# Another order for the first transfers of an attention-and-MLP kernel, and decoding of weights from its first step

## The chip, the cores and the metric

The kernel runs on one NeuronCore of a Trainium2 chip, as one launch. The metric is the device time of the launch in microseconds (us). TensorE (PE) multiplies matrices, VectorE (DVE) and ScalarE (ACT) work on whole tiles, GpSimd (POOL) only sets up constants here, and SyncE (SP) issues most of the transfers. PEld is the loading of weights into the PE array.

## What is computed

The inputs are q, k, v and a complex decay a, of 4 batches, 8 heads, 768 positions and 48 channels. A state of 48x48 per head is decayed and added to at every position, and two MLPs follow on the 3072 tokens of width 384, with a hidden width of 2048:

```
scale = min(|a|, 0.999) / (|a| + 1e-6);  a = a * scale          # complex
for t in range(768):
    S = a[t] * S + outer(k[t], v[t]);  y[t] = q[t] @ real(S)
x = y as (3072, 384)
x = softplus(x @ w_in1) @ w_out1
out = elu(x @ w_in2) @ w_out2
```

The MLP weights arrive as float64 and are used as pairs of float32 parts (high and low), so each product is three matmuls.

## The kernel before

**Attention.** The sequence is cut into 12 units of 256 positions (3 to a batch). For a unit u, `load_a` fetches the real and imaginary decays, `load_qk` q and k, `load_v` v by halves. `norm` (L143) makes the scale of the decays: squares on ACT, a sum on DVE, Ln and Exp on ACT, then DVE and ACT in turn. `prep` (L175) forms the running products W of the decays on DVE, first `W<-ar` and `W<-ai` (L183, L185). `qk` (L232) multiplies them into q (QP, the tile `big<-W,qr`) and divides k by them (KP, `big<-W,tmp`, L267). KP is stored to DRAM as `kd` (L271) and read back in another layout as `KN` (L327); PE waits for KN before it updates the state (L395). `chunks` (L799) issues scores (L334), the causal mask on DVE (tile P, L340), outputs (L358, L361) and a relay into the layout of the first MLP (L384). What it leaves is X[u], as a high and a low part (`xh` and `xl`, L404 and L405).

**Weights.** A granule is a 128x384 float64 block, 384 KB; the first MLP has 32 of them, the second 32 more. `w_load` (L487) fetches one, an even one from w_in, an odd one from w_out. `w_step` (L507) decodes one: on ACT an Abs and an Exp that test the range (L445, L446), on DVE three integer operations (L449, L451, L452), then ACT copies the high part (L404) and DVE subtracts it (L405). Here granule g is written g0, g1 and so on.

**Order.** A generator `stream()` hands out the attention in steps. Until X[0] is there, one weight granule is handed out with each step once `step > S0`, until G0 = 22. Thereafter the first MLP runs in 8 pieces per unit (n = 0 to 95, `a_s1` at L528, `a_elem` at L538 with DVE's L545 and L550) with attention handed out in between, and from unit 11 on the second MLP follows. The order in which these are issued is a first order only: a scheduler that plays the program through with costs of its own moves the instructions of each engine. The engines then work in that order, and each waits in it. SP issues in order too: its transfers take eight completion semaphores in turn, so a transfer waits for the one eight places ahead.

Before, the first transfers are the decays of unit 0, its q and k, two halves of v, the decays of unit 1, and then granules 0 to 7 (L938 to L944).

Of the kernel before, what the change touches and what calls it, by code (L numbers as in the profile page):

```python
# [411 lines left out]

CH0 = 7
DLY = 2
S0 = 6
STEP = 2000
STEPS = 4
G0 = 22
# [6 lines left out]
LA = 8  # L425
# [328 lines left out]
def body(tc, q, k, v, a_re, a_im, w_in1, w_out1, w_in2, w_out2, out):  # L754
    nc = tc.nc
    keep = tc.tile_pool(name="keep", bufs=1)
    with keep as keep:
        fine = quick(tc, keep, q, k, v, a_re, a_im, w_in1, w_out1, w_in2, w_out2, out)
        n = nc.values_load(fine[0:1, 0:1], min_val=0, max_val=128)
        with tc.If(n < 128):  # L760
            general(tc, q, k, v, a_re, a_im, (w_in1, w_out1, w_in2, w_out2), out)


def quick(tc, keep, q, k, v, a_re, a_im, w_in1, w_out1, w_in2, w_out2, out):
    nc = tc.nc
    with ExitStack() as ctx:
# [13 lines left out]
        net = Net(tc, ctx, flags[:, 28:92], bank, ((w_in1, w_out1), (w_in2, w_out2)))  # L780
# [4 lines left out]
        A = Attn(tc, actx, flags, bank, net, q, k, v, a_re, a_im)  # L785
# [136 lines left out]
        def adv(ns):  # L922
# [3 lines left out]
            for _ in range(STEPS):  # L926
# [5 lines left out]
                try:  # L932
# [2 lines left out]
                    due = A.vec.ns  # L935
                    return

        A.load_a(0)  # L938
        A.load_qk(0)
        A.load_v(0)  # L940
        A.load_v(1)
        A.load_a(1)
        for net.top in range(LA):
            net.w_load(net.top)  # L944
        while 0 not in X:
            next(st)
            if net.g < G0 and step > S0:
                net.w_step()
# [130 lines left out]
```

## Time and profile before

| | us |
|---|---|
| median of 3 runs | 1166.83 |
| lowest and highest of them | 1163.89, 1168.22 |
| the profiled execution | 1162.61 |
| its span, from first to last instruction | 1160.8 |
| PE, DVE, ACT busy | 1001.1, 810.4, 667.2 |

Busy times overlap, and instructions that follow each other on an engine overlap a little too. The profile also names for each idle stretch what ended it, and follows a chain of waits back from the last instruction; rows called "issue" in it are time in which nothing that the profile shows was waited for.

### The profile page before, as it was taken

What the parts mean: (1) busy time and instruction counts of PE and PEld (TensorE: products, weight loads), DVE (VectorE), ACT (ScalarE), POOL (GpSimd) and SP (SyncE); (2) the same over time, 40 slices, a digit from 0 to 9 for tenths busy, and PEclk for the clock granted to TensorE, in tenths of its full rate; (3) what the DMA queues carried; (4) which work ended last, traced back from release to release, by engine and by line L of the source; (5) the groups of instructions that cost most, each with busy time, mean ns of one, the idle gap of its engine ahead of it and who ended that gap; (6) DMA issues with size and microseconds to landing.
All of it is one profiled execution on the core that took longest, in us unless ns stands there. A gap on an engine that the chain in (4) does not pass through costs nothing.

```text
span 1160.8 us, 18255 instructions
## 1 busy us (share of the span) xinstructions
PE 1001.1 (86%) x7106; PEld 933.2 (80%) x7106; DVE 810.4 (70%) x1521; ACT 667.2 (57%) x1207; POOL 2.2 (0%) x20
## 2 busy tenths in 40 slices
PE   0015988898999797997999899999999999999997
PEld 0014888888988797897999899999999999999996
DVE  3997999798987889796989978983434343333332
ACT  4735865565746565474656578974545454454443
POOL 0000000000000000000000000000000000000000
PEclk9996999999998899898999999999999999999999
DMA  7536262343634435472546365530101000000000
GB/s 205 182 116 161 91 171 76 89 140 88 175 96 116 118 108 175 98 204 56 179 108 210 83 205 187 160 117 1 55 1 55 1 1 28 1 28 1 29 1 30
DMA packets 101823, 114.51 MB, mean 99 GB/s; under 512 B 49760, under 2 KB 78944, under 8 KB 101728
## 3 DMA queue, kind: packets, MB, share of 16 engines
q1 hardware_dynamic: 90272, 105.40, 31.6%
q10 hardware_dynamic: 11456, 7.87, 2.2%
q8 instruction: 57, 0.93, 0.3%
q14 instruction: 38, 0.31, 0.1%
HBM read 77.86 MB, written 35.39 MB: 98 GB/s over the span
## 4 chain that ended last, share of the span: by engine, by line
PE 58%; DMA 16%; DVE 13%; ACT 8%; issue 4%; SPq 2%; ACTq 0%; DVEq 0%
PE b L525 49%; DMA kd<-big 4%; DMA KN<-kd 4%; DVE big L28 3%; PE b L334 3%; DVE tmp L28 3%; PE b L395 2%; PE b L358 2%; DMA wr<-in_moe_w_out_dram 1%; ACT w L446 1%; ACT w L445 1%; DMA wr<-in_moe_w_in_dram 1%; PE b L361 1%; DVE W L28 1%; DMA kT<-dk 1%
## 5 line engine op out<-in xcount | busy, mean ns | idle before, releaser
L525 PE MATMUL b<-xh,w 128*128 128x256 f32 (+1 forms) x1728 | 405.6, 328 | 32.3 <-ACT xh L404 25.3
L525 PEld LDWEIGHTS b<-xh,w 128*128 128x128 f32 x1728 | 293.9, 197 | 55.5 <-ACT xh L404 27.7
L525 PE MATMUL b<-xl,w 128*128 128x256 f32 (+1 forms) x864 | 278.9, 326 | 0.1
L525 PE MATMUL b<-gh,w 128*128 128x256 f32 x1152 | 213.4, 286 | 1.7 <-ACT gh L548 1.6
L525 PE MATMUL b<-w,gh 128*128 128x384 f32 x768 | 191.1, 335 | 0.0
L525 PEld LDWEIGHTS b<-gh,w 128*128 128x128 f32 x1152 | 176.9, 193 | 4.4 <-ACT gh L548 2.5
L525 PEld LDWEIGHTS b<-xl,w 128*128 128x128 f32 x864 | 167.5, 195 | 13.2 <-DVE xl L405 0.7
L584 DVE SCALAR_TENSOR_TENSOR t<-t,b 128x512 f32<-128x512 f32 x96 | 66.0, 687 | 151.1 <-ACT t L582 151.1
L525 PE MATMUL b<-gl,w 128*128 128x256 f32 x576 | 156.0, 286 | 1.4 <-DVE gl L550 1.4
L525 PEld LDWEIGHTS b<-w,gh 128*128 128x128 f32 x768 | 139.9, 188 | 7.8
L525 PE MATMUL b<-w,gl 128*128 128x384 f32 x384 | 124.2, 335 | 0.0
L581 ACT ACTIVATE t<-b 128x512 f32<-128x512 f32 x96 | 57.2, 597 | 111.1 <-PE b L525 110.3
L405 DVE TENSOR_TENSOR gl<-t,gh 128x512 fp32r<-128x512 f32 x96 | 66.4, 692 | 72.0 <-ACT gh L404 70.9
L525 PEld LDWEIGHTS b<-gl,w 128*128 128x128 f32 x576 | 106.5, 192 | 3.0 <-DVE gl L550 2.2
L404 ACT ACTIVATE gh<-t 128x512 fp32r<-128x512 f32 x96 | 60.6, 632 | 78.0 <-PE b L525 72.0
L541 ACT ACTIVATE t<-b 128x512 f32<-128x512 f32 x96 | 56.8, 593 | 66.5 <-PE b L525 56.2
L296 PE MATMUL b<-eye,big 128*96 128x128 f32 x112 | 19.3, 320 | 86.8 <-DVE big L28 86.5
L548 ACT ACTIVATE gh<-t 128x512 fp32r<-128x512 f32 x96 | 60.0, 627 | 55.5 <-PE b L525 37.2
L296 PEld LDWEIGHTS b<-eye,big 128*96 128x96 f32 x112 | 14.8, 147 | 88.5 <-issue 85.5
L525 PEld LDWEIGHTS b<-w,gl 128*128 128x128 f32 x384 | 71.7, 188 | 0.1
L550 DVE TENSOR_TENSOR gl<-t,gh 128x512 fp32r<-128x512 f32 x96 | 65.4, 685 | 8.1 <-ACT gh L548 7.0
L545 DVE SCALAR_TENSOR_TENSOR t<-b,t 128x512 f32<-128x512 f32 x96 | 65.5, 683 | 5.6 <-ACT t L543 5.4
(114 smaller groups left out, 1440.6 us busy)
## 6 DMA issues: line engine op xcount, KB each, us to landing
wr<-in_moe_w_in_dram SPq DMA_DIRECT2D x32, 384.0 KB
wr<-in_moe_w_out_dram SPq DMA_DIRECT2D x32, 384.0 KB
dq<-big SPq DMA_DIRECT2D x12, 768.0 KB
qT<-dq SPq DMA_DIRECT2D x36, 256.0 KB
kd<-big SPq DMA_DIRECT2D x12, 768.0 KB
KN<-kd SPq DMA_DIRECT2D x20, 384.0 KB
ar<-in_a_re_dram SPq DMA_DIRECT2D x12, 384.0 KB
ai<-in_a_im_dram SPq DMA_DIRECT2D x12, 384.0 KB
```

Of the source, the lines that this page charges most:

```text
L28: return f(*a, **kw)
L296: nc.tensor.transpose(out=ps[0:96, 128 * i:128 * i + 128], in_=W[:, 96 * (4 * g + i):96 * (4 * g + i) + 96], identity=self.eye)
L334: self.nc.tensor.matmul(out=sc[:, h, :], lhsT=KT[:, 4 * g + h, :], rhs=QT[:, 4 * g + h, :], start=(h == 0), stop=(h == 3), skip_group_chec ...
L404: nc.scalar.activation(out=hi, in_=x, func=AF.Copy)
L405: nc.vector.tensor_tensor(out=lo, in0=x, in1=hi.bitcast(F32), op=ALU.subtract)
L525: self.nc.tensor.matmul(out=out, lhsT=lhsT, rhs=rhs, skip_group_check=True, **kw)
L541: nc.scalar.activation(out=t, in_=h, func=AF.Abs)
L545: nc.vector.scalar_tensor_tensor(out=t, in0=h, scalar=0.0, in1=t, op0=ALU.max, op1=ALU.add)
L548: nc.scalar.activation(out=gh, in_=t, func=AF.Copy)
L550: nc.vector.tensor_tensor(out=gl, in0=t, in1=gh.bitcast(F32), op=ALU.subtract)
L581: nc.scalar.activation(out=t, in_=h, func=AF.Relu, scale=-1.0)
L584: nc.vector.scalar_tensor_tensor(out=t, in0=t, scalar=-1.0, in1=h, op0=ALU.add, op1=ALU.max)
```

## The change

The first transfers are issued in another order: granule 0, the decays of unit 0, granules 1 to 4, the decays of unit 1, granules 5 to 7, then q and k and two halves of v. And S0 is 0, so that decoding is handed out from the first step on. Nothing is added or left out.

```diff
-S0 = 6
+S0 = 0
...
+        net.w_load(0)
         A.load_a(0)
+        for net.top in range(1, 5):
+            net.w_load(net.top)
+        A.load_a(1)
+        for net.top in range(5, LA):
+            net.w_load(net.top)
         A.load_qk(0)
         A.load_v(0)
         A.load_v(1)
-        A.load_a(1)
-        for net.top in range(LA):
-            net.w_load(net.top)
```

What it moves is seen in three places. SP's first transfers (wr is a granule as it arrives, ar and ai are decays), before:

```order
L96 DMA ar_143<-in_a_re_dram 128x1x768
L96 DMA ai_145<-in_a_im_dram 128x1x768
L106 DMA qr_147<-in_q_dram 128x1x768
L106 DMA kr_149<-in_k_dram 128x1x768
L112 DMA V0_137<-in_v_dram 128x8x48
L112 DMA V1_139<-in_v_dram 128x8x48
L96 DMA ar_153<-in_a_re_dram 128x1x768
L96 DMA ai_155<-in_a_im_dram 128x1x768
L496 DMA wr_157<-in_moe_w_in_dram 128x3x128
```

and now:

```order
L496 DMA wr_143<-in_moe_w_in_dram 128x3x128
L96 DMA ar_145<-in_a_re_dram 128x1x768
L96 DMA ai_147<-in_a_im_dram 128x1x768
L494 DMA wr_149<-in_moe_w_out_dram 128x384
L496 DMA wr_151<-in_moe_w_in_dram 128x3x128
L494 DMA wr_153<-in_moe_w_out_dram 128x384
L496 DMA wr_155<-in_moe_w_in_dram 128x3x128
L96 DMA ar_157<-in_a_re_dram 128x1x768
L96 DMA ai_159<-in_a_im_dram 128x1x768
L494 DMA wr_161<-in_moe_w_out_dram 128x384
```

Granules 6 and 7, q, k and the two halves of v follow, and then granule 8. DVE's first instructions behind its memsets (tmp is the scale of unit 0, f and w are a granule in decoding), before:

```order
L28 SCALAR_TENSOR_TENSOR tmp_173<-tmp_173,tmp_174 128x768
L28 TENSOR_TENSOR tmp_174<-tmp_173,tmp_175 128x768
L28 SCALAR_TENSOR_TENSOR tmp_174<-tmp_174,tmp_175 128x768 x2
L449 TENSOR_SCALAR f_202<-wr_157 128x384
L28 SCALAR_TENSOR_TENSOR en_301<-en_301,en_302 128x768
L28 SCALAR_TENSOR_TENSOR tmp_173<-tmp_173,tmp_174 128x768
L451 SCALAR_TENSOR_TENSOR f_202<-wr_157,f_202 128x384
L449 TENSOR_SCALAR f_219<-wr_159 128x384
L28 TENSOR_TENSOR W_187<-ar_143,tmp_173 128x16x48
```

and now:

```order
L449 TENSOR_SCALAR f_179<-wr_143 128x384
L451 SCALAR_TENSOR_TENSOR f_179<-wr_143,f_179 128x384
L452 SCALAR_TENSOR_TENSOR f_179<-wr_143,f_179 128x384
L405 TENSOR_TENSOR w_178<-f_179,w_178 128x384
L28 SCALAR_TENSOR_TENSOR tmp_173<-tmp_173,tmp_174 128x768
L449 TENSOR_SCALAR f_193<-wr_149 128x384
L449 TENSOR_SCALAR f_206<-wr_151 128x384
L451 SCALAR_TENSOR_TENSOR f_193<-wr_149,f_193 128x384
L451 SCALAR_TENSOR_TENSOR f_206<-wr_151,f_206 128x384
L452 SCALAR_TENSOR_TENSOR f_193<-wr_149,f_193 128x384
L452 SCALAR_TENSOR_TENSOR f_206<-wr_151,f_206 128x384
L28 TENSOR_TENSOR tmp_174<-tmp_173,tmp_175 128x768
```

Five granules are decoded there ahead of `W<-ar`, where before there were three instructions of two granules. The third place is ACT's first instructions behind its table load (en is the scale of unit 1), before:

```order
L148 ACTIVATE tmp<-ar 128x768
L149 ACTIVATE tmp<-ai 128x768
L152 ACTIVATE tmp<-tmp 128x768
L153 ACTIVATE tmp,flags<-tmp 128x768
L156 ACTIVATE tmp<-tmp,flags 128x768
L148 ACTIVATE en<-ar 128x768
L159 ACTIVATE tmp<-tmp,flags 128x768
L149 ACTIVATE en<-ai 128x768
L445 ACTIVATE w<-wr 128x384
```

and now:

```order
L445 ACTIVATE w<-wr 128x384
L446 ACTIVATE w,flags<-w 128x384
L148 ACTIVATE tmp<-ar 128x768
L404 ACTIVATE w<-f 128x384
L149 ACTIVATE tmp<-ai 128x768
L445 ACTIVATE w<-wr 128x384
L446 ACTIVATE w,flags<-w 128x384
L152 ACTIVATE tmp<-tmp 128x768
L445 ACTIVATE w<-wr 128x384
L153 ACTIVATE tmp,flags<-tmp 128x768
L445 ACTIVATE w<-wr 128x384
L446 ACTIVATE w,flags<-w 128x384
```

The tests of the granules now stand between the steps of the scale of unit 0.

## Rows read from the trace of the kernel before

**Rows 1.** Page, parts 1 and 2: busy share of the span, and in 40 slices.
```profile
PE 1001.1 (86%) x7106; PEld 933.2 (80%) x7106; DVE 810.4 (70%) x1521; ACT 667.2 (57%) x1207; POOL 2.2 (0%) x20
...
PE   0015988898999797997999899999999999999997
...
DVE  3997999798987889796989978983434343333332
```

**Rows 2.** Windows: busy us of PE, PEld, DVE, ACT, POOL, clock, DMA share, GB/s.
```profile
23.40:80.40 57.00, 0.00 (x0) 0.00 (x0) 56.47 (x127) 31.87 (x82) 0.00 (x0) 1.00 0.48 163
80.40:117.50 37.10, 22.46 (x156) 17.74 (x156) 30.21 (x77) 20.81 (x44) 0.00 (x0) 0.73 0.64 172
117.50:188.40 70.90, 62.94 (x514) 57.78 (x514) 67.33 (x144) 48.63 (x93) 0.00 (x0) 0.95 0.38 107
188.40:780.00 591.60, 541.77 (x4552) 518.75 (x4553) 515.62 (x969) 381.58 (x691) 0.00 (x0) 0.95 0.48 137
...
sum 1137.40, PE 1001.13 PEld 933.17 DVE 806.42 ACT 659.07 POOL 0.00; mean PE 200.23 PEld 186.63 DVE 161.28 ACT 131.81 POOL 0.00
```

**Rows 3.** Timeline to 30 us: start, us, instruction, idle before it and its releaser.
```profile
0.83 0.80 SPq L96 DMA_DIRECT2D ar<-in_a_re_dram  x1
...
3.71 4.94 SPq L112 DMA_DIRECT2D V<-in_v_dram  x2
6.17 0.84 ACT L148 ACTIVATE tmp<-ar 128x768 f32<-128x768 f32 x1 [4.06 <-DMA ar<-in_a_re_dram]
8.69 5.08 SPq L96 DMA_DIRECT2D ar<-in_a_re_dram  x1
8.86 0.84 ACT L149 ACTIVATE tmp<-ai 128x768 f32<-128x768 f32 x1 [1.84 <-DMA ai<-in_a_im_dram]
...
18.78 0.84 ACT L148 ACTIVATE en<-ar 128x768 f32<-128x768 f32 x1 [4.22 <-DMA ar<-in_a_re_dram]
...
20.48 0.96 DVE L28 SCALAR_TENSOR_TENSOR tmp<-tmp 128x768 f32<-128x768 f32 x1 [5.97 <-ACT tmp L159]
...
23.44 0.36 DVE L449 TENSOR_SCALAR f<-wr 128x384 int32<-128x384 int32 x1 [2.00 <-DMA wr<-in_moe_w_in_dram]
...
27.06 0.95 DVE L28 TENSOR_TENSOR W<-ai,tmp 128x768 f32<-128x768 f32 x1
```

**Rows 4.** Windows, same columns: transfers of weights, and one of q alone.
```profile
25.00:30.00 5.00, 0.00 (x0) 0.00 (x0) 5.00 (x9) 5.00 (x15) 0.00 (x0) 1.00 1.05 373
...
70.00:71.00 1.00, 0.00 (x0) 0.00 (x0) 1.00 (x2) 1.00 (x3) 0.00 (x0) 1.00 0.48 187
```

**Rows 5.** Chain in order of time, to 80 us: start, us, what.
```profile
67.69 0.47 DVE f L451
68.15 0.27 DVE f L449
...
78.76 1.68 DVE big L28
```

**Rows 6.** Chain, behind 80 us: store and reload of unit 0.
```profile
80.46 6.13 DMA kd<-big
86.60 8.05 DMA KN<-kd
...
188.44 0.60 DVE t L545
```

**Rows 7.** Timeline of the first unit behind the reload: DVE and PE.
```profile
94.79 2.76 PE L395 MATMUL b<-V,KN 128*96 128x48 f32 x16 [6.83 <-DMA KN<-kd]
96.90 0.36 DVE L449 TENSOR_SCALAR f<-wr 128x384 int32<-128x384 int32 x1 [3.35 <-DMA wr<-in_moe_w_out_dram]
...
101.41 0.69 DVE L28 TENSOR_TENSOR P<-b,mask 128x512 f32<-128x512 f32 x1 [2.61 <-PE b L334]
```

**Rows 8.** Timeline, same: second half of unit 0 and the first matmul.
```profile
106.55 0.68 DVE L28 TENSOR_TENSOR P<-b,mask 128x512 f32<-128x512 f32 x1
...
117.54 1.65 PE L525 MATMUL b<-xh,w 128*128 128x256 f32 x6 [0.58 <-ACT xh L404]
```

## The prediction

> **What bounds the kernel now.** I read the shares of the span first. Over the whole, PE is busiest (86%), but the slices show two parts: in the last third PE is full and DVE at a third, while before that DVE is nearly full and in the first three slices, to 80 us, PE does nothing [rows 1]. A stage-by-stage table of busy time then says who sets the pace of the start. DVE is busy 56.5 of 57.0 us from 23.4 to 80.4, when the first keys are ready to be stored; 30.2 of 37.1 to the first MLP matmul at 117.5; and 67.3 of 70.9 to 188.4, where the first elementwise step of unit 1 stands [rows 2, 6, 8]. From there to 780 PE is busy 542 and DVE 516 of 592: both are near full, and the chain goes through both.
>
> Ahead of 23.4 us DVE is nearly idle. Of its 810.4 us in all, 806.4 lie behind that point, so 4.0 are ahead of it and 19.4 are idle [rows 1, 2]. The timeline shows why: the decays of unit 0 arrive at 6.2 and 8.9, then two halves of v hold up SP's issue (4.94 us for the two, and 5.08 for the transfer behind them). ACT, in its order, stands at the square of the decays of unit 1 until 18.8, with the last step of unit 0's scale behind it, for which DVE waits 5.97 us; and the first granule is there only at 23.4 [rows 3]. So the start is bound by when things arrive, and from 23.4 on by DVE.
>
> **The change, part by part.** No instruction is added or removed; what counts is what lies in the idle 19.4 us and what is pushed back.
>
> *When granule 0 arrives.* Decays alone move 384 KB (0.393 MB) at the rate of q alone, 187 GB/s: 2.10 us. Weights run at 373 GB/s: 1.05 us [rows 4]. The first transfer now takes 1.05 in place of 2.10 and starts at the same time, so granule 0 is there at 6.17 - 1.05 = 5.1 us [rows 3]. The decays of unit 0 come 1.05 later: 7.2, and 2.7 behind that (8.86 - 6.17) 9.9. Granules 1 to 4 follow at 1.05 each, 11.0 to 14.1, and the decays of unit 1 at some 18 to 20, about where the first half of them was. The Trainium skill, in "DMA: Bandwidth & Descriptors" (Anatomy of one DMA), gives 2.0 us plus the bytes at 436 GB/s for one transfer, fitted on the GpSimd path; that is 2.9 us, granule 0 at 3.7 and 1.4 us more gain. The first transfer of this trace took 5.3 us to its first use, so I go by the row.
>
> *What fits in.* One granule costs DVE 0.27 + 3 x 0.47 = 1.68 us, the integer operations and the subtraction alike [rows 5]. Ahead of `W<-ar` now stand five whole granules, 8.4 us, where before two L449 and one L451 stood, 1.0 us: 17 instructions or 7.4 us more. Walking DVE and ACT through the new order with these arrivals: granule 0 to 6.8; the scale's sum at 10.8 (the decays at 9.9 and a square of 0.84); granules 1 and 2 to 14.5, the next two steps of the scale to 16.4, granules 3 and 4 to 20.1, then the waits for ACT, whose tests of the granules (some 1 us each) now stand between the steps of the scale. `W<-ai` of unit 0 then ends at about 26, against 27.06 + 0.95 = 28.0 [rows 3]. So DVE is 2 us earlier with 7.4 us more done: 9.4 us ahead.
>
> *The first keys.* From `W<-ai` to the keys KP of unit 0 the order has 58 decoding instructions before and now (61 - 3 and 78 - 20). So KP starts about 2 us earlier, at 76.8 instead of 78.76 [rows 5]. Its store and reload, 6.13 + 8.05 us [rows 6], stay: the SP queue now has one granule more between the reload of q and the store and one between the store and the reload of the keys, 1.05 us each at most, and POOL's queue has nothing.
>
> *Behind the keys.* Up to X[0] DVE has 25 decoding instructions left instead of 35, and the scheduler puts 28 others ahead of it instead of 44. In that stretch DVE waited 6.9 us (37.1 - 30.2), for a granule (3.35) and for PE, which itself waited for KN (6.83), and the masks of the second half came 5.1 us apart with decoding between them [rows 2, 7, 8]. With less between, I expect the first MLP matmul at 109 to 111 instead of 117.5. Not all of that stays, since the 16 other instructions still stand behind it.
>
> *What stays.* At the first L545 of unit 1 both orders have the same ahead of it: 128 decoding instructions, 198 of the attention, 26 others. There the lead is the idle time saved. The 9.4 us shrink by what DVE waits more for the unchanged round trip of the keys, because it has 7.4 us less of decoding to put into it; some of the work of unit 1 fills it. I take a quarter, 2.4 us: less than the 7.4, since the order already puts `W<-ar` of unit 1 and what follows it into the trip, and not nothing, since DVE waited 6.9 us there even with that decoding. **7 us** remain at 181 instead of 188.4. From there on the instructions are the same, and PE and DVE are as near to full as before, so the shift reaches the end.
>
> Bounds: DVE's idle time from 5.1 to 23.4, less 4.0 of work and less the 2.7 between the two decays, is 11.6 us; more can't be won there. The least, while the lead in decoding counts for nothing, is the 2 us by which the keys are earlier, less 1 for the granule that shares the reload.
>
> Against the profiled execution: 1162.6 - 7 = 1155.6 us. It is 4.2 below the median of the runs, so the median goes from 1166.8 to **1159.8**.
>
> **The rivals.**
>
> *The round trip sets it (0.17).* Keys 2 us earlier, and everything behind them follows PE's waits and not DVE's work: gain 1 to 4.5, about 1164. For it: PE's wait of 6.83 for KN, and PE's granted clock, 0.73 on the mean of that stretch and so part of it at the lower of its levels of 1.2 and 2.4 GHz, after 80 us without work. Against it: DVE is 95% busy from 117.5 to 188.4 [rows 2, 7].
>
> *ACT stands in its order (0.09).* Granules 8 to 18 now come behind q, k and v on SP. ACT tests them in order, and the L404 of earlier granules and a step of unit 1's scale stand behind those tests. The row at 20.48 shows what that does: DVE waited 5.97 us for a ready step that was queued behind a late transfer [rows 3]. If the two halves of v hold SP for about 10 us as they do now, granule 8 comes at 27 to 28 and granule 18 at 38 to 39, about when ACT gets there; each us beyond that is a us of DVE. Three to six us late gives 1160 + 4 to 7, so 1164 to 1169. "TensorE: Matmul & The Clock Gate" of the Trainium skill (its table at the head) calls ScalarE's and VectorE's queues strict first-in, first-out; by that rule nothing behind such a test can pass it, and the wait at 20.48 agrees.
>
> *Slower: decoding in front of the keys, without cover (0.06).* The order has 17 decoding instructions more ahead of KP. If none of the 19.4 idle us is used, because granules 1 to 4 arrive only with the decays of unit 1, they lie on the path: KP 7.4 us later, the round trip with it, and the time 1171 to 1174. It decides from granule 4 arriving at about 20 us on. For it: the first transfers run at 187 GB/s, not 373, when only decays are under way; at that rate all of granules 1 to 4 take 8.4 us and end at 18.3. Against: weights reach 373 [rows 4].
>
> **The numbers.** A measurement of this kernel can tell about 0.5%, 5.8 us. The forecast (4.5 to 11.6 won) has 0.68, of which I put four fifths, 0.54, beyond 5.8 won. The round trip, ACT's order and a small loss stay within it: 0.14 + 0.17 + 0.10 = 0.41; 0.05 is slower by more. The forecast and the round trip hold 0.85 and reach from 11.6 to 1 won, 1155.2 to 1165.8; with a little for the runs' own spread (2.9 below to 1.4 above their median) I take 1154 to 1167.
>
> **What would show it.** In the profile after: the first L449 at about 5 us; DVE busy some 15 of its first 26 us; `W<-ai` of unit 0 ending near 26; KP starting near 77; the first L525 near 110 and the first L545 of unit 1 near 181; the stage from there to the end as long as now. It is wrong if `W<-ai` ends behind 28, if ACT is idle before an L445 between 25 and 45 us with DVE idle too, or if the lead is there at 181 and gone at the end.

## The result, and the profile of the changed kernel

The changed kernel takes **1178.12 us** (median of 4 runs, 1178.04 to 1178.49) against 1165.80 for the kernel before on the same chip (1163.89 to 1168.22): a ratio of 1.0105, 95% interval 1.0084 to 1.0126. It is slower by 12.3 us. The forecast was 1159.8, with a range to 1167.

The profiled execution has a span of 1176.5 us. Its page answers to [rows 1]: the same work, PE still at 86%, a fuller DVE in the first slice (5 against 3) and emptier ones at once behind it (7 against 9 in the second, 5 against 7 in the fourth).

```profile
PE 1007.0 (86%) x7106; PEld 938.9 (80%) x7106; DVE 811.6 (69%) x1521; ACT 668.9 (57%) x1207; POOL 2.2 (0%) x20
...
PE   0006888899896989697899999999999999999997
...
DVE  5795996889998879896889988983434333343332
```

The windows of the changed kernel, cut at its own landmarks (the store of the first keys at 87.8, the first L525 at 125.4, the first L545 of unit 1 at 203.2), answer to [rows 2]. The columns are busy us of PE, PEld, DVE, ACT and POOL, the clock, the DMA share and GB/s; behind them stand two stretches of the transfers and two at the end of unit 1's keys.

```profile
0.00:23.00 23.00, 0.00 (x0) 0.00 (x0) 10.84 (x25) 13.43 (x27) 2.25 (x20) 1.00 0.81 186
23.00:60.00 37.00, 0.00 (x0) 0.00 (x0) 29.52 (x70) 22.25 (x57) 0.00 (x0) 1.00 0.61 187
60.00:87.80 27.80, 0.00 (x0) 0.00 (x0) 27.80 (x58) 9.02 (x17) 0.00 (x0) 1.00 0.32 95
87.80:125.40 37.60, 26.45 (x157) 21.66 (x157) 22.55 (x53) 17.29 (x36) 0.00 (x0) 1.00 0.63 159
125.40:203.20 77.80, 65.67 (x506) 60.84 (x507) 68.24 (x150) 47.78 (x91) 0.00 (x0) 0.87 0.32 93
...
2.00:10.00 8.00, 0.00 (x0) 0.00 (x0) 1.78 (x4) 2.54 (x6) 0.93 (x9) 1.00 0.94 192
35.00:45.00 10.00, 0.00 (x0) 0.00 (x0) 3.86 (x10) 8.48 (x22) 0.00 (x0) 1.00 1.02 362
...
184.00:188.00 4.00, 2.84 (x19) 2.85 (x20) 1.37 (x3) 1.10 (x2) 0.00 (x0) 0.74 0.09 24
188.00:192.00 4.00, 4.00 (x27) 2.63 (x28) 1.17 (x6) 0.53 (x2) 0.00 (x0) 0.50 0.26 49
```

The first two stretches of the kernel before, to compare:

```profile
0.00:23.00 23.00, 0.00 (x0) 0.00 (x0) 3.95 (x7) 7.71 (x10) 2.24 (x20) 1.00 0.63 161
23.00:60.00 37.00, 0.00 (x0) 0.00 (x0) 36.07 (x95) 26.71 (x74) 0.00 (x0) 1.00 0.58 204
```

Take the length of each stretch less DVE's busy time, and the loss can be placed. DVE's idle us, by stage:

| | to the store of the keys | to the first L525 | to the first L545 of unit 1 | sum |
|---|---|---|---|---|
| before | 20.0 | 6.9 | 3.6 | 30.5 |
| changed | 19.6 | 15.0 | 9.6 | 44.2 |

The idle time that the change aimed at is still there, 0.4 us less. DVE is busy 6.9 us more up to 23 us (10.84 against 3.95 in the same window of before) and 6.6 less from 23 to 60 (29.52 against 36.07). But 14 us of new idle time stand behind the keys. Behind 203.2 little more is lost: from there to the last instruction are 973.3 us, against 972.4 before.

The stage from the store of the keys to the first L525 is as long as before (37.6 against 37.1), but DVE has 22.55 us of work in it where it had 30.21 [rows 2]. By the traces these are 24 decoding instructions and 28 others, where 34 and 41 stood.

The timeline shows the waits. It answers to [rows 3] and [rows 7]; each row has start, length, instruction, and in brackets the idle time before it and what ended it.

```profile
4.10 0.36 DVE L449 TENSOR_SCALAR f<-wr 128x384 int32<-128x384 int32 x1 [3.09 <-DMA wr<-in_moe_w_in_dram]
...
8.41 0.84 ACT L148 ACTIVATE tmp<-ar 128x768 f32<-128x768 f32 x1 [3.11 <-DMA ar<-in_a_re_dram]
...
9.70 0.56 DVE L405 TENSOR_TENSOR w<-f,w 128x384 fp32r<-128x384 f32 x1 [4.05 <-ACT w L404]
...
12.64 0.84 ACT L149 ACTIVATE tmp<-ai 128x768 f32<-128x768 f32 x1 [2.98 <-DMA ai<-in_a_im_dram]
13.51 0.96 DVE L28 SCALAR_TENSOR_TENSOR tmp<-tmp 128x768 f32<-128x768 f32 x1 [3.26 <-ACT tmp L149]
...
17.39 9.37 SPq L112 DMA_DIRECT2D V<-in_v_dram  x2
...
26.80 5.80 SPq L496 DMA_DIRECT2D wr<-in_moe_w_in_dram  x1
...
28.58 0.95 DVE L28 TENSOR_TENSOR W<-ai,tmp 128x768 f32<-128x768 f32 x1
...
36.11 0.56 ACT L445 ACTIVATE w<-wr 128x384 fp32r<-128x384 f32 x1 [5.02 <-DMA wr<-in_moe_w_in_dram]
...
42.97 0.56 DVE L405 TENSOR_TENSOR w<-f,w 128x384 fp32r<-128x384 f32 x1 [5.67 <-ACT w L404]
...
106.03 2.80 PE L395 MATMUL b<-V,KN 128*96 128x48 f32 x16 [6.96 <-DMA KN<-kd]
...
111.92 0.69 DVE L28 TENSOR_TENSOR P<-b,mask 128x512 f32<-128x512 f32 x1 [7.96 <-PE b L334]
...
185.16 1.40 PE L334 MATMUL b<-qT,kT 96*128 96x128 f32 x8 [2.25 <-ACT ye L367]
```

Granule 0 is there at 4.10 and decoded at once, but its last step (L405) waits 4.05 us for ACT, which stands at the decays until 8.41. Granule 8, issued at 26.80 behind v, is tested at 36.11, and the L405 at 42.97 has waited 5.67 behind that. At 111.92 DVE stands 7.96 us at the first mask P for the scores.

The chain of waits, in order of time, answers to [rows 5, 6]: KP starts at 85.99, 7.2 us late, and store and reload have grown to 8.07 + 10.07.

```profile
85.99 1.77 DVE big L28
87.78 8.07 DMA kd<-big
95.91 10.07 DMA KN<-kd
...
203.28 0.60 DVE t L545
```

DVE's waits behind the keys, in us in total, times, and the longest:

```profile
DVE P L28 <- PE b L334: 11.2, 3, 8.0
DVE w L405 <- ACT w L404: 1.9, 2, 1.5
...
DVE P L28 <- PE b L334: 4.7, 2, 2.8
DVE xl L405 <- ACT xh L404: 4.0, 2, 3.2
```

The first two are of the stage to 125.4, the others of the one to 203.2. Nearly all the new idle time is DVE standing at a mask, or at xl, for PE and ACT. Before, it stood there 2.6 us in the first of these stages and 2.1 in the second:

```profile
DVE P L28 <- PE b L334: 2.6, 1, 2.6
...
DVE xl L405 <- ACT xh L404: 1.9, 2, 1.0
...
DVE P L28 <- PE b L334: 0.2, 1, 0.2
```

### The profile page after: what moved, and what is told of

Read it like the earlier page. It is cut to its first block, busy times and chain, and to the rows that moved or that the text cites. A ratio compares the mean times of both kernels' runs of the same rounds, so it can differ in the third digit from the quotient of the medians.

```text
span 1176.5 us, 18261 instructions
## 1 busy us (share of the span) xinstructions
PE 1007.0 (86%) x7106; PEld 938.9 (80%) x7106; DVE 811.6 (69%) x1521; ACT 668.9 (57%) x1207; POOL 2.2 (0%) x20
## 4 chain that ended last, share of the span: by engine, by line
PE 61%; DMA 15%; DVE 12%; ACT 5%; issue 3%; SPq 3%; ACTq 0%; DVEq 0%
PE b L525 52%; PE b L334 4%; DVE tmp L28 3%; DMA wr<-in_moe_w_out_dram 3%; DMA xr<-xd 3%; DVE big L28 2%; DMA KN<-kd 2%; DMA kd<-big 2%; PE b L358 2%; PE b L395 2%; DMA kT<-dk 1%; DMA ar<-in_a_re_dram 1%; DMA xd<-ye 1%; DVE W L28 1%; PE b L361 1%
## 5 line engine op out<-in xcount | busy, mean ns | idle before, releaser
L525 PE MATMUL b<-xh,w 128*128 128x256 f32 (+1 forms) x1728 | 404.9, 328 | 33.9 <-ACT xh L404 28.1
L525 PEld LDWEIGHTS b<-xh,w 128*128 128x128 f32 x1728 | 293.9, 196 | 55.7 <-ACT xh L404 30.0
L525 PE MATMUL b<-xl,w 128*128 128x256 f32 (+1 forms) x864 | 278.3, 325 | 0.3
L525 PE MATMUL b<-gh,w 128*128 128x256 f32 x1152 | 216.7, 288 | 2.2 <-ACT gh L548 2.2
L525 PE MATMUL b<-w,gh 128*128 128x384 f32 x768 | 191.4, 335 | 0.0
L525 PEld LDWEIGHTS b<-gh,w 128*128 128x128 f32 x1152 | 178.4, 193 | 5.9 <-ACT gh L548 3.3
L525 PEld LDWEIGHTS b<-xl,w 128*128 128x128 f32 x864 | 166.9, 195 | 12.8 <-DVE xl L405 0.9
L525 PE MATMUL b<-gl,w 128*128 128x256 f32 x576 | 157.1, 287 | 3.0 <-DVE gl L550 3.0
L525 PEld LDWEIGHTS b<-w,gh 128*128 128x128 f32 x768 | 140.0, 188 | 7.8
L525 PE MATMUL b<-w,gl 128*128 128x384 f32 x384 | 124.3, 335 | 0.0
L405 DVE TENSOR_TENSOR gl<-t,gh 128x512 fp32r<-128x512 f32 x96 | 66.4, 692 | 72.3 <-ACT gh L404 70.9
L525 PEld LDWEIGHTS b<-gl,w 128*128 128x128 f32 x576 | 107.6, 193 | 4.3 <-DVE gl L550 3.4
L296 PE MATMUL b<-eye,big 128*96 128x128 f32 x112 | 18.7, 306 | 91.1 <-DVE big L28 87.9
L548 ACT ACTIVATE gh<-t 128x512 fp32r<-128x512 f32 x96 | 60.0, 626 | 45.2 <-DVE t L545 20.9
L525 PEld LDWEIGHTS b<-w,gl 128*128 128x128 f32 x384 | 71.7, 188 | 0.2
L545 DVE SCALAR_TENSOR_TENSOR t<-b,t 128x512 f32<-128x512 f32 x96 | 65.4, 683 | 7.8 <-ACT t L543 7.6
```

The source lines that it names most:

```text
L296: nc.tensor.transpose(out=ps[0:96, 128 * i:128 * i + 128], in_=W[:, 96 * (4 * g + i):96 * (4 * g + i) + 96], identity=self.eye)
L405: nc.vector.tensor_tensor(out=lo, in0=x, in1=hi.bitcast(F32), op=ALU.subtract)
L525: self.nc.tensor.matmul(out=out, lhsT=lhsT, rhs=rhs, skip_group_check=True, **kw)
L545: nc.vector.scalar_tensor_tensor(out=t, in0=h, scalar=0.0, in1=t, op0=ALU.max, op1=ALU.add)
L548: nc.scalar.activation(out=gh, in_=t, func=AF.Copy)
```

## The experiments

**Theory**, in this account: the keys are late since 17 decoding instructions more stand ahead of them, and no idle time was saved to pay for those; DVE then has too little left to decode while the keys travel. Since the edit moves only transfers, that order is the scheduler's, which seems to count on the granules early. **Rival**: the transfers cost by themselves, since decays mixed with granules make both late. In the expectations the two names change sides: for e1 to e5, e7 and e14 "theory" is that the transfers' own times decide (v holding SP, mixed kinds) and "rival" the decoding ahead of the keys; for e13 and from e16 on it is as here. Times are medians; ratios are to the kernel before on the same chip. That kernel's own executions lie between 1158 and 1175, so single traces are read for places and not for totals.

### Each half of the change alone

`e1` is the changed kernel with `S0 = 6`, `e2` the kernel before with `S0 = 0`.

> The new transfer order with S0 back at 6. Theory (the transfers do it: the two halves of v hold SP, granule 8 arrives at 36 us and ACT and DVE stand behind it): as slow as the change, 1176 to 1180 us. Rival (handing out decoding from the first step puts decoding ahead of the first keys): most of the 12 us come back, 1166 to 1170 us. The scheduler's order on every engine is the same as in the change but for buffer names, which speaks for the theory.

> S0 = 0 alone, with the transfers in the order of before. Theory (transfers): the same as before, within 0.3%, 1163 to 1169 us. Rival (decoding from the first step): slower by 5 to 12 us, 1171 to 1178 us.

Measured: e1 1178.97 (1.0100, 1.0065 to 1.0136), e2 1165.15 (0.9993, 0.9973 to 1.0014). S0 does nothing: in both cases every engine's order stays the same but for buffer names. The whole loss comes with the order of the transfers.

The two traces also show how well one order repeats. DVE's idle time is 19.5 and 7.0 us in the first two stages for e2 (20.0 and 6.9 before) and 19.7 and 15.2 for e1 (19.6 and 15.0 in the change), but 6.6 in the third for e2 (3.6 before) and 13.1 for e1 (9.6 in the change). Their third stages, e1 first:

```profile
125.54:206.91 81.37, 66.48 (x506) 61.14 (x507) 68.24 (x151) 48.01 (x91) 0.00 (x0) 0.85 0.32 89
...
117.38:191.22 73.84, 67.03 (x514) 62.01 (x514) 67.24 (x144) 48.66 (x93) 0.00 (x0) 0.89 0.37 103
```

So the 8 us lost in the trip of the keys are firm, while the 6 of the next stage are less than twice what two executions of one order differ by.

### Where v goes

`e3` takes the change and issues v later (behind granule 15 by SP's trace; the expectations say 13); `e4` issues its first two halves on ACT's queue; `e5` does e3's edit on the kernel before.

```diff
-        A.load_v(0)
-        A.load_v(1)
+        A.nv = False
...
+            if net.g == 8 and not A.nv:
+                A.load_v(0)
+                A.load_v(1)
+                A.nv = True
```

> The change with the two halves of v issued behind granule 13 instead of ahead of granule 8. Theory (v holds SP): granule 8 is there before 27 us, DVE's wait of 5.7 us for a high part behind ACT's test goes, the first keys start 5 to 7 us earlier than in the change (79 to 81 us) and the time is 1170 to 1173 us. Rival (the decoding that now stands ahead of the keys, four granules or 7 us): the keys stay at 84 to 86 us and the time at 1175 to 1179 us.

> The change with the two halves of v issued from ACT's queue at the start. Theory (v holds SP): as with v late, granule 8 before 27 us, keys at 79 to 81 us, 1170 to 1173 us, if ACT's own issue of v (its first work) costs nothing. Rival (decoding ahead of the keys): 1175 to 1179 us. A third outcome: v moves early on the same 16 engines and delays the first decays, keys at 83 to 85 us.

> The kernel before with only the two halves of v moved: they are issued behind granule 13 instead of in front of the decays of unit 1. Theory (the start is bound by when transfers come, and v holds SP for some 10 us there): the first L449 comes at 13 to 16 instead of 23.4, KP at 71 to 75 instead of 78.7 and the time falls to 1157 to 1162. Rival (what lies ahead of the keys on DVE and ACT sets them, v does not): the first L449 comes earlier but KP stays at 77 to 79 and the time at 1163 to 1168.

Measured: e3 1169.59 (1.0040, 1.0004 to 1.0076), but by another way than expected: KP stays at 85.92, and granule 8, which SP issues 9.7 us earlier (17.08), is tested only 1.1 us earlier (35.03). So v on SP is not what made it late. DVE's idle time in the first trip of the keys falls from 15.0 to 7.4, with as many decoding instructions ahead of the keys as in the change (78), since the scheduler put more of the rest there, 82 instructions and not 53:

```profile
87.71:126.35 38.64, 25.16 (x156) 20.33 (x156) 31.20 (x82) 23.04 (x53) 0.00 (x0) 0.96 0.68 188
```

So the decoding ahead of the keys does not by itself empty the trip; what counts is the work that the order leaves in it.

e4 1170.08 (1.0026, 0.9994 to 1.0057), with KP even later, 91.7. e5 1179.96 (1.0102, 1.0052 to 1.0152): as slow as the change and beyond both expectations, on the old transfers but for v, with KP at 79.6, within 1 us of before. So neither v on SP nor the time of KP alone explains the times. All three also have an order of their own from the scheduler, which these runs do not separate from their transfers.

### Transfers sorted by kind

`e7` loads the decays of units 0 and 1, granules 0 to 7, then q, k and v; `e14` adds e3's edit.

> The changed kernel with its first transfers sorted by kind: decays of units 0 and 1, then granules 0 to 7, then q, k and v; 72 decoding instructions stand ahead of KP. Theory (transfers that use half of the engines, mixed with granules, made both late): decays of unit 0 at 6.2 and 8.9 as before the change, granule 0 at 13 to 15 and the next ones about 1.1 apart, KP at 75 to 79, time 1157 to 1164. Rival (decoding ahead of the keys costs its 0.43 us each wherever the granules come): KP at 82 to 84 and the time 1168 to 1173.

> As e7_unmixed, and the two halves of v behind granule 13 as well; 70 decoding instructions ahead of KP. Theory (when transfers come decides): granules 8 and on no longer wait behind v, KP 1 to 3 us earlier than in e7_unmixed, time 1155 to 1161, the fastest of these. Rival: no earlier than e7_unmixed, 1163 to 1170.

Measured: e7 1172.53 (1.0062, 1.0032 to 1.0093), KP at 82.0; e14 1187.82 (1.0165, 1.0121 to 1.0210), KP at 84.7. The first L449 came at 17.1 and 18.3, later than expected. e7 came out as decoding ahead of the keys would have it (82 to 84, 1168 to 1173). e14 is 18 us above the higher of its ranges. So unmixing does not bring the time back: e14 mixes less than the change and is 10 us slower.

### Decoding pinned ahead of the keys, or behind them

Here an instruction is held behind another one of its engine in the issue order, with no wait added. `e13`: the change, with granules 15 and on fetched and decoded behind KP.

```diff
-            if net.g < G0 and step > S0:
-                net.w_step()
+            if net.g < G0 and step > S0 and (net.g < 15 or A.key):
+                net.late(A.key)
...
+    def late(self, ins):
+        with (self.tc.issue_after(ins) if ins is not None else nullcontext()): self.w_step()
```

`e17`: the kernel before, with granules up to 19 ahead of KP (S0 is 0 in it, in `e18` and in `e20`, which did nothing in e2). `e16`: the change, with 15 granules ahead of KP, fetched as usual, 7 behind it, and the first P behind those. `e18` and `e20`: the kernel before, with 12 or 15 granules ahead, the others to 21 behind KP, and P behind those.

> The changed kernel, its first transfers untouched as far as granule 14, but the decoding of granule 15 and of those behind it is pinned behind KP of unit 0 on DVE, and those granules are fetched with that, so 59 decoding instructions stand ahead of KP (61 before the change, 78 with it). Theory (the keys are late because 17 instructions more stand ahead of them and no idle time was saved): KP at 77 to 80 and the time back to 1163 to 1168, since that decoding then fills the round trip of the keys. Rival (late granules and decays themselves hold DVE and ACT up, whatever the order): KP at 83 or later and the time above 1172.

> The kernel before with its own first transfers, but KP of unit 0 on DVE is pinned behind the decoding of granule 19, and granules 20 and 21 behind KP: 78 decoding instructions ahead of the keys, as in the changed kernel, instead of 61. Theory (what costs is that decoding is gone when DVE should fill the round trip of the keys; the transfers are only the way in which the scheduler came to it): KP at 85 to 87, DVE waits over 6 us for the scores of unit 0, first L545 of unit 1 at 198 or later, time 1172 to 1182 as with the change. Rival (the mix of first transfers costs by itself): the same work in another order on a DVE that is full costs little, first L545 of unit 1 at 187 to 193, time 1163 to 1169.

> The changed kernel with all its transfers, but the decoding of granules 15 to 21 pinned behind KP of unit 0 on DVE, and the first mask P of unit 0 pinned behind that decoding: 59 decoding instructions ahead of the keys, 7 granules in their round trip. Theory: KP at 76 to 80, DVE waits less than 2 us for the scores of unit 0 (11.2 in the changed kernel), first L545 of unit 1 at 187 to 193, time 1160 to 1168. Rival (the mix of first transfers costs by itself): KP at 77 to 80 as in the run with the cap, first L545 of unit 1 still at 200 or later, time above 1173.

> The kernel before with its transfers; only 12 granules are decoded ahead of KP of unit 0 (47 instructions instead of 61), granules 12 to 21 are pinned behind it, and the first mask P of unit 0 behind those. Theory: KP 14 x 0.43 = 6 us earlier, at 72 to 74, the round trip is full of decoding, no wait for the scores of unit 0 on DVE, time 1155 to 1163, less than before. Rival: PE, which gets P later, sets it: first L525 later than 117.5, time 1168 or more.

> The kernel before with its transfers; 59 decoding instructions ahead of KP of unit 0 as before (61), granules 15 to 21 pinned behind it and the first mask P behind those. Theory: as before the change up to KP (78 to 79), DVE's 2.6 us of waiting for the scores of unit 0 gone, time 1160 to 1166. Rival (P later on PE sets it): first L525 at 120 or later, time 1168 or more.

Measured: e13 1190.48 (1.0179, 1.0125 to 1.0233). KP came at 77.0 as the theory said, and the time went the other way, to where its rival had it (above 1172): an early KP is not worth anything by itself. Of the 36 us by which its trace is longer than that of before, 22 lie behind the first L545 of unit 1; why is not shown. e17 1173.93 (1.0051, 1.0006 to 1.0096): with the old transfers, 78 decoding instructions ahead of KP make the keys as late as in the change (87.3), and DVE stands behind them, as the theory had it. The waits of e17 from the keys to the first L545 of unit 1:

```profile
DVE P L28 <- PE b L334: 16.7, 6, 7.8
DVE xl L405 <- ACT xh L404: 8.4, 3, 4.9
```

So an order alone can cost time without the new transfers, by the ratio about half of what the change costs. The traced execution was the slowest of its six (1180.89), so its waits are large for it.

e16 1174.52 (1.0057, 1.0024 to 1.0090) missed the theory's 1160 to 1168 and lies where the rival had it (above 1173); its profiled execution was the slowest of its ten, so its trace decides nothing here. e18 1170.27 (1.0027, 1.0001 to 1.0054) and e20 1171.31 (1.0062, 1.0033 to 1.0090) are misses for the theory: KP came at 72.8 and 76.0, but the first L525 only at 125.9 and 120.1, since P had been put behind more decoding than the trip lasts. That was the rival of these two.

### Two orders on two sets of transfers

The cleanest separation: a list of instruction numbers fixes the whole order of DVE, ACT and PE, and the transfers are chosen apart from it. `e21`: new transfers, every instruction of these engines in the order of the kernel before. `e23` and `e24`: old and new transfers with an edited order. On ACT, L159 of unit 0 goes ahead of L148 of unit 1; on DVE the attention up to KP goes 13 places ahead of the decoding; PE keeps its order.

```diff
+def pin(nc, tc):
+    have = {i.name: i for i in nc.cur_bb.bb.instructions}
+    for names in json.loads(zlib.decompress(base64.b85decode(ORDER))):
+        line = [have[f"I-{n}"] for n in names if f"I-{n}" in have]
+        for a, b in zip(line, line[1:]):
+            tc.add_manual_dep(b, a.name, mybir.DependencyInfo(
+                mybir.DependencyClass.NoSync, mybir.DependencyReason.DATA), reason="pin")
```

> The changed kernel's first transfers, with every instruction of DVE, ACT and PE pinned to the order that the kernel before has (S0 = 6). Theory (the loss is the order that the scheduler makes of the new transfers, not the transfers): KP of unit 0 at 77 to 81, first L545 of unit 1 at 187 to 192, time 1162 to 1169. Rival (mixed transfers, late decays and late granules cost by themselves): KP at 83 or later, first L545 of unit 1 at 196 or later, time 1173 or more.

> The kernel before with its own transfers and its order on PE, and two moves in the order of the others: on ACT the last step of the scale of unit 0 (L159) stands ahead of the squares of the decays of unit 1, and on DVE the products of unit 0 start behind that scale at once, 13 instructions of them ahead of the first granule's decoding; from there on the order is as before, with the attention 13 places ahead of the decoding, so 41 decoding instructions ahead of KP instead of 61 and 20 more behind it. Theory (the idle 20 us at the start are lost by the order in which DVE and ACT stand, and decoding is what fills the round trip of the keys): W<-ar at 16 to 18 instead of 26.2, KP at 61 to 66, first L525 at 102 to 109, time 1150 to 1158, less than both kernels. Rival (the round trip or ACT sets what follows): KP as early, but first L545 of unit 1 at 184 or later and the time 1160 or more.

> The changed kernel's first transfers with the orders of DVE, ACT and PE of the run before this one. Theory (orders decide, transfers move little): W<-ar at 20 to 23, since the decays come 2.2 and 3.8 us later than before the change, KP at 65 to 71, time 1153 to 1162, within 6 us of the run before this one and less than the changed kernel by 15 or more. Rival (the mixed transfers cost by themselves): more than 8 us above the run before this one.

| median us (ratio to before, interval) | old transfers | new transfers |
|---|---|---|
| order of before | 1167.32 | 1169.28 (1.0018, 0.9992 to 1.0044) |
| edited order | 1159.47 (0.9920, 0.9892 to 0.9947) | 1163.41 (0.9967, 0.9945 to 0.9990) |

Windows of e21, cut at the same landmarks, with the columns as above:

```profile
23.00:79.80 56.80, 0.00 (x0) 0.00 (x0) 55.95 (x126) 31.36 (x80) 0.00 (x0) 1.00 0.46 148
79.80:116.70 36.90, 27.17 (x157) 21.91 (x157) 30.38 (x76) 20.86 (x44) 0.00 (x0) 0.94 0.63 170
116.70:187.50 70.80, 63.93 (x507) 58.92 (x508) 67.32 (x144) 48.19 (x93) 0.00 (x0) 0.91 0.39 107
```

The lengths and the busy times of DVE and ACT are those of [rows 2] within 1 us, with KP at 78.0; PE's busy time in the second stretch differs (27.17 against 22.46) without changing its length. **The new transfers, late decays included, cost 2.0 us as long as the order is the old one, with an interval from -0.9 to 5.1.** The decays of unit 0 are 2.2 and 3.1 us late in e21 too, but granule 8 is not: it is tested at 32.77, against 33.48 before and 36.11 in the change. The same transfers in the scheduler's order cost 1.05%, 12.3 us. So most of the loss is the order's, and the rival is left with 5 of the 12 us at most. On the edited order the new transfers cost 3.9 us, and the two intervals overlap only from 0.9945 to 0.9947: there `W<-ar` starts at 21.7 and not at 18.0, and KP, the first L525 and the first L545 of unit 1 all come 2.8 later.

The pin holds three orders at once. By the traces, the change has another instruction than the kernel before at 871 of DVE's 1521 places, 624 of ACT's 1207 and 2417 of PE's 7106. No run takes the three apart, so how much of the loss is DVE's empty trip, and how much the order of PE or ACT, is argued and not shown.

The edited order beats both kernels, by 8 us (0.53% to 1.08%) on the old transfers. Its timeline at the start:

```profile
15.03 0.93 ACT L159 ACTIVATE tmp<-tmp,flags 128x768 f32<-128x768 f32 x1
...
17.99 0.96 DVE L28 TENSOR_TENSOR W<-ar,tmp 128x768 f32<-128x768 f32 x1
...
19.40 0.84 ACT L148 ACTIVATE en<-ar 128x768 f32<-128x768 f32 x1 [3.43 <-DMA ar<-in_a_re_dram]
```

`W<-ar` starts at 18.0 instead of 26.2. And its windows:

```profile
0.00:19.80 19.80, 0.00 (x0) 0.00 (x0) 6.72 (x10) 7.01 (x9) 2.24 (x20) 1.00 0.58 143
19.80:72.40 52.60, 0.00 (x0) 0.00 (x0) 47.14 (x105) 30.68 (x78) 0.00 (x0) 1.00 0.59 188
72.40:113.00 40.60, 25.22 (x156) 20.91 (x156) 38.95 (x96) 23.27 (x49) 0.00 (x0) 0.98 0.59 164
113.00:184.50 71.50, 63.23 (x514) 57.92 (x514) 67.61 (x144) 48.71 (x93) 0.00 (x0) 0.94 0.39 107
```

Even here the idle time to the keys is 18.5 us (13.1 + 5.5). What fell is the idle time of the trip, from 6.9 to 1.6, since 20 decoding instructions more are left for it. The expectation had KP at 61 to 66, the first L525 at 102 to 109 and 1150 to 1158; they came at 70.6 and 113.0, and the time is 1.5 above that range. The first L545 of unit 1, at 184.4, is where the rival had it. e24 missed likewise, with KP at 73.4 and a time 1.4 above its range, but is within 6 us of e23 as expected; e21's time is 0.3 above its range, its KP and L545 are inside. The trace places 3.9 us of the gain up to the first L545 of unit 1 (184.4 against 188.4). Where the other 4 lie is not shown.

DVE's idle us by stage in the other runs (e16 left aside), in the order of their sum, with the ratio of the time to before:

| | to the keys' store | to the first L525 | to unit 1's L545 | sum | ratio |
|---|---|---|---|---|---|
| e23 | 18.5 | 1.6 | 3.9 | 24.0 | 0.9920 |
| e24 | 21.5 | 1.7 | 3.9 | 27.1 | 0.9967 |
| e20 | 18.0 | 6.6 | 4.5 | 29.1 | 1.0062 |
| e21 | 19.2 | 6.5 | 3.5 | 29.2 | 1.0018 |
| e3 | 19.7 | 7.4 | 4.6 | 31.7 | 1.0040 |
| e2 | 19.5 | 7.0 | 6.6 | 33.1 | 0.9993 |
| e18 | 19.4 | 9.5 | 6.0 | 34.9 | 1.0027 |
| e7 | 18.5 | 11.2 | 7.1 | 36.8 | 1.0062 |
| e4 | 22.1 | 6.6 | 11.3 | 39.9 | 1.0026 |
| e13 | 17.8 | 11.5 | 14.5 | 43.8 | 1.0179 |
| e14 | 22.1 | 14.7 | 7.6 | 44.4 | 1.0165 |
| e1 | 19.7 | 15.2 | 13.1 | 48.0 | 1.0100 |
| e5 | 18.7 | 12.2 | 18.3 | 49.2 | 1.0102 |
| e17 | 20.9 | 11.3 | 19.8 | 52.0 | 1.0051 |

Whatever is done to order or transfers, the first column stays between 17.4 and 22.1 in all seventeen traces. The second and third move, and the time broadly with them. Not all of it lies there: behind the first L545 of unit 1 the traces of e13 and e14 are 22 and 12 us longer than that of before, and those of e7 and e17 are 8 and 7 shorter.

## Why the prediction was wrong, step by step

- *When granule 0 arrives.* 5.1 was said, 4.10 measured. The Trainium skill's fit in "DMA: Bandwidth & Descriptors" (Anatomy of one DMA), which gave 3.7, was nearer than the row: 3.27 us from issue to first use, against its 2.9.
- *The decays of unit 0*, "1.05 later: 7.2, and 2.7 behind that", 9.9. Measured 8.41 and 12.64. I added one granule's 1.05 us at the full rate, but up to eight transfers are in flight at once (SP has issued nine by 5.59, of which granule 0 has landed): from 2 to 10 us the engines are 94% busy and move only 192 GB/s. Granules 1 to 4 were tested at 13.5 to 17.9, where 11.0 to 14.1 was said; granule 8 at 36, not 27 to 28.
- *What fits in.* "So DVE is 2 us earlier with 7.4 us more done: 9.4 us ahead" failed. `W<-ai` ended at 29.5 instead of 26, behind the 28 that the prediction itself named as a sign of being wrong, and by 60 us DVE had worked 40.36 us, against 40.02 before. I walked the first 26 us and stopped: the next waits (granule 8, and an L405 behind ACT) gave the rest back.
- *The first keys.* From that, KP at 76.8; it came at 85.99. With the idle time unchanged, the 17 instructions are 17 x 0.43 = 7.3 us, and KP is 7.2 late.
- *Behind the keys.* "The 9.4 us shrink by what DVE waits more for the unchanged round trip [...] I take a quarter, 2.4 us". **This is the step that cost most.** DVE waits 8.1 us more in that trip and 6.0 more in the next stage: 14 us, more than the whole lead. I saw that 7.4 us less of decoding was left for the trip, and then took less than that. I also let the stretch shrink with DVE's work in it ("the first MLP matmul at 109 to 111"). It did not: with 7.7 us less work for DVE it took 37.6 us, against 37.1, and the first L525 is as late as the keys, 7.9 and 7.2 us. The trip is also not unchanged: 18.1 us instead of 14.2, where one more granule between store and reload was priced at 1.05.
- *What stays.* "The shift reaches the end" held: 14.8 us at the first L545 of unit 1, 15.7 in the span.
- *Bounds.* The lower bound, a gain of 1, left out that the lead can be negative.
- *The slower rival*, "decoding in front of the keys, without cover" at 1171 to 1174, named the first half of the mechanism, keys later by 7.4, and got 0.06. Its condition (granule 4 arriving at about 20) was not met, for granule 4 was tested at 17.9, and it decided all the same: the idle time does not have to stay at the start, it only has to come back before the keys. Its price was short by the second half of the loss. *ACT stands in its order* was true too (5.02 and 5.67 us): part of how the idle time came back. The rule that ScalarE's and VectorE's queues are strict first-in, first-out ("TensorE: Matmul & The Clock Gate" of the Trainium skill, the table at its head) agrees with both waits.
- *The round trip sets it* had it that what is behind the keys follows PE's waits and not DVE's work. Up to the first L525 that came true: DVE had less to do, and the first matmul still followed the keys. What it had wrong was keys 2 us earlier. PE's wait for KN by itself is as before, 6.96 against 6.83.

The loss in the stage to the first L545 of unit 1 has one more part that the runs do not separate from the order: PE's clock. From 184 to 188 PE is busy 2.84 of 4 us, with 2.25 us idle before the scores at 185.16, and the granted clock is then 0.50, that is 1.2 GHz, from 188 to 192, with PE full and DVE mostly idle. Over the whole stage the clock is 0.87 on the mean, against 0.95 before. As an estimate from these means and the two levels, some 20 us of the stage are at the lower level, against 7. e1 and e2 have 0.85 and 0.89 there, and longer stages than the same orders had in the change and before; but e21, with the order of before, has 0.91 and the same length. In e5 it is seen for longer: PE is full at 0.50 from 180 to 190 us, and DVE works 1.31 us of these ten.

## What to carry to other kernels

Before counting idle time at the start as a gain, follow one engine's idle time, stage by stage, to a point where the same work is done: filling one gap early can take filler from a later one, and here the later gap was larger. Where the distance of two points is set by a transfer and another engine, less work between them is idle time and not a gain. When a scheduler with costs of its own sits between edit and program, a change of transfers is a change of every engine's order; pin the order and vary the transfers, or the other way round, before blaming either. The order itself was worth more than the transfers: two moves in it gained 8 us, and the new transfers cost 2 to 4 on a fixed order.

## What the runs showed of the hardware that was not expected

- Decays and granules in flight together moved 192 GB/s at a share of 0.94 from 2 to 10 us, against 362 GB/s at 1.02 from 35 to 45, where it is nearly all granules; q alone had 187 at only 0.48 [rows 4]. The engines are as busy as with granules and move half as much; why is not shown.
- Two halves of v hold SP's issue for 9.37 us here, with granules in flight (1.18 of them, from 19.46 to 20.64, are a wait for the decays eight places ahead), and the transfer behind them for 5.80; before it was 4.94 and 5.08 [rows 3].
- Granule 8, for which ACT stood waiting each time, was tested 9.3 us behind its issue in the change, and 18.0 behind it in e3, where SP issued it 9.7 us earlier.
- The new transfers made the decays of unit 0 late by 2.2 and 3.8 us and granule 8 by 2.6. With the old order they cost 2.0 us, not clear of zero (e21), and with the edited order 3.9 (e24).
